# 1/z of a head pair by DMA broadcast in place of six transposes, and GpSimd made to wait for VectorE

## The chip, the cores and the metric

The kernel runs on one NeuronCore of a Trainium2 chip. The metric is the device time of one execution in microseconds (us), lower is better. A change of less than about 0.2% (1.3 us here) can hardly be told from none.

## The reference

Inputs are q, k and v of shape (2, 8, 768, 64), a random projection of 6 columns, and the weights of two feed-forward blocks of 512 channels. Attention is masked by hash buckets: a query sees only the keys whose projected sign bits equal its own. Each row is divided by its sum z.

```python
scores = np.where(mask, scale * q @ k.T, -1e9)
attn = np.exp(scores - scores.max(-1))
attn = attn / (attn.sum(-1) + 1e-9)
x = heads_side_by_side(attn @ v)             # (2, 768, 512)
h = relu(x @ w_in); u, v = halves(h)         # gated block
y = (u * (w_spatial @ layernorm(v) + b)) @ w_out
out = y + relu(layernorm(y) * g @ w1) @ w2
```

## The kernel before

The program has three parts. Part 0 is attention, with the projections of the first batch's gated block mixed in towards its end; parts 1 and 2 are the rest of the gated block and the second block. Attention works on 96 tiles of 128 queries, `order` in the code: 2 batches of 8 heads of 6 tiles. For a tile, TensorE makes the scores (`sc`), VectorE takes the masked minimum into `x` (signs are turned, so it is a row maximum), ScalarE takes the exponential in place and adds up the row sums into `z_sum`, TensorE transposes `x` in six blocks (`pt`), ScalarE and VectorE copy these to `e`, and after a head's sixth tile 24 matmuls (`po`) make the head's output, which two copies put into `xT`. `xT` holds channels on the partitions (two heads of 64 make one slice of 128) and queries on the columns. It is not yet divided by z.

The division is done for a pair of heads by two functions that `attn_step` calls. `summed` (line 895), one tile behind the pair's last `po`, takes 1/(z + 1e-9) into `zr`, where queries are on the partitions. `normalized` (line 902), three tiles behind, turns it: GpSimd spreads `zr` over 64 columns for each head (`zw`), TensorE transposes three blocks of 128x128 into `pz`, and VectorE multiplies `xT` by `pz`; that for both halves of the 768 queries, so six transposes for a pair and 48 for the eight pairs. Who reads `xT` is `x_split` (line 1038), which makes the operand `act_x` of the gated block's projections `pv`.

No instruction is issued in the order in which these functions call it. Each call is recorded as a job of the class `Plan`; `Plan.run` (line 298) plays the jobs against modelled costs, picks for each engine which job comes next, and `Plan.issue` (line 477) issues all jobs in the planned order of their start; each engine then runs its own in that order. So every edit deals the whole order anew, that of parts 1 and 2 too. Every job is issued by one line, 499, so the profile's rows are told apart by tile names. In the plan a VectorE job marked `shared` (its operands are all in SBUF) and a GpSimd job do not overlap; nothing makes the chip keep to that, since GpSimd runs ahead if its own inputs are there.

Loads of queries and keys (`qs`, `ks`), of `vv` and all reloads are issued by SyncE's queue (SP), in order; the raw weights and stores of weight pieces by ScalarE's queue. TensorE's outputs in attention go to `ps_s` (2 buffers of scores) and `ps_b` (4 banks, for `pt`, `po`, `pm` and `pz`).

Of the kernel before, what the change touches and what calls it, by code (L numbers as in the profile page):

```python
# [9 lines left out]
F32 = mybir.dt.float32  # L10
# [4 lines left out]
ALU = mybir.AluOpType  # L15
# [3 lines left out]
P = 128  # L19
# [124 lines left out]
class Job:  # L144
    def __init__(self, at, engine, part):
        self.at, self.engine, self.part = at, engine, part
        self.calls, self.after, self.busy, self.lag, self.bytes = [], set(), 0.0, 0.0, 0
        self.start = self.end = None
        self.shared = self.closed = False


# [18 lines left out]
class Plan:  # L170
# [4 lines left out]


    RUN = 6
    LOOK = 55
    EARLY = 20.0
    BULK = 14.0  # L180
# [117 lines left out]
    def run(self, late=None):  # L298
# [27 lines left out]
        def done(j):  # L326
            stack = [j]
            while stack:
                j = stack.pop()
                for h in heirs[j]:  # L330
                    if j.engine is None:
                        t = j.end
                    elif h.engine == j.engine and not j.bytes:
                        t = j.start + j.busy if h.engine in ("PE", "SP") else j.end + self.NEXT
                    else:
                        t = j.end + self.HOP.get(h.engine, 0.0)
                        if h.bytes and h.engine == "ACT":
                            t += self.SLACK
                    ready[h] = max(ready[h], t)
                    left[h] -= 1  # L340
                    if not left[h]:
                        if h.engine is None:
                            h.start = h.end = ready[h]
                            stack.append(h)
                        else:
                            known[h.engine].append(h)
# [5 lines left out]
        while todo:  # L352
            best = None
            for force, e in [(f, e) for f in (False, True) for e in engines]:
                if force and best:
                    break
                live = [p for p, n in parts[e].items() if n]
# [3 lines left out]
                c = [j for j in known[e] if j.part == part]  # L361
                if e != "PE" and not force:
                    c = [j for j in c if opened(j) is not None]
# [4 lines left out]
                t = max(free[e], min(ready[j] for j in c))  # L368
# [4 lines left out]
            t, e, c = best  # L373
# [103 lines left out]
    def issue(self):  # L477
        self.gates()
        self.settle()
        order = sorted((j for j in self.jobs if j.engine), key=lambda j: (j.part, j.start, j.at))  # L480
        engine = {"PE": "tensor", "ACT": "scalar", "DVE": "vector", "POOL": "gpsimd", "SP": "sync"}
        nc = self.tc.nc
        live = lambda x: x.real() if isinstance(x, View) else x
        opened = {}
        part = -1
        def opening(p):
            for pool in self.pools:
                if pool.part == p:
                    stack = opened.setdefault(pool.how.pop("till", None), ExitStack())
                    pool.real = stack.enter_context(self.tc.tile_pool(name=pool.name, bufs=pool.bufs, **pool.how))  # L490
        with self.tc.manual_schedule():
            for j in order:
                while part < j.part:
                    part += 1
                    if part in opened:
                        opened.pop(part).close()
                    opening(part)
                for op, args, kw in j.calls:
                    getattr(getattr(nc, engine[j.engine]), op)(*map(live, args), **{k: live(x) for k, x in kw.items()})  # L499
            for stack in reversed(list(opened.values())):  # L500
                stack.close()

# [2 lines left out]
def attn_moe_kernel(ctx: ExitStack, tc: tile.TileContext, qT, kT, v, proj, w_in, w_spT, b_sp, w_out, g_ln, w1, w2, out):  # L505
# [166 lines left out]
    xT = {}  # L672
# [221 lines left out]

    def summed(b, r):

        zr = ap.tile([P, NQT, 2], F32, tag="zr", name=f"zr_{b}_{r}")
        nc.vector.tensor_scalar(zr, z_sum[b][:, :, 2 * r : 2 * r + 2], 1e-9, None, op0=ALU.add)
        nc.vector.reciprocal(zr, zr)
        pairs[b, r]["zr"] = zr  # L900

    def normalized(b, r):

        zr = pairs[b, r]["zr"]
        for c in range(2):
            zw = ap.tile([P, 6, D], F32, tag="zw", name=f"zw_{b}_{r}_{c}", bufs=2)
            zc = zr[:, c * 3 : c * 3 + 3, :].rearrange("p a (h o) -> p (a h) o", o=1)
            nc.gpsimd.tensor_scalar(zw, zc.to_broadcast([P, 6, D]), 1.0, 0.0, op0=ALU.mult, op1=ALU.add)
            pz = ps_b.tile([P, 3, P], F32, tag="b", name=f"pz_{b}_{r}_{c}")
            for i in range(3):  # L910
                nc.tensor.transpose(pz[:, i, :], zw[:, 2 * i : 2 * i + 2].rearrange("p h d -> p (h d)"), ident)
            xs = xT[b][:, r, c * KC : (c + 1) * KC]
            nc.vector.tensor_tensor(xs, pz.rearrange("p a n -> p (a n)"), xs, op=ALU.mult)

    def attn_step(i):
# [11 lines left out]
            exps(*order[i + 1])  # L927
        if 0 <= i - PO < NT and order[i - PO][2:] == (NG - 1, GRP - 1):
            weighted(*order[i - PO][:2])
        for late, e in ((1, summed), (3, normalized)):  # L930
            n = i - PO - late
            if 0 <= n < NT and order[n][1] % 2 == 1 and order[n][2:] == (NG - 1, GRP - 1):
                e(order[n][0], order[n][1] // 2)
        n = i + 1 + QA
# [728 lines left out]
```

## Time and profile before

| | |
|---|---|
| time before, median of 3 runs | 649.05 us (648.55 to 649.79) |
| the profiled execution: its own time | 648.87 us |
| its span in the trace | 646.9 us |
| TensorE busy | 637.4 us (99%) |
| VectorE busy | 508.1 us (79%) |
| ScalarE busy | 326.4 us (50%) |
| GpSimd busy | 193.8 us (30%) |

The profiled execution's time is 1.97 us more than its span; that lies around the instructions. Matmuls are pipelined and their ends are modelled, so a busy TensorE may hold short pauses. PE is TensorE's matmul, PEld its weight load, DVE is VectorE, ACT ScalarE, POOL GpSimd, and SPq and ACTq are DMA issues on the queues of SyncE and ScalarE.

### The profile page before, as it was taken

The numbers are of one execution on the slowest core, as the hardware profiler recorded it, in microseconds if no ns is written. First come the engines' busy times: TensorE is split into PE (matmuls) and PEld (weight loads), VectorE is DVE, ScalarE is ACT, GpSimd is POOL, SyncE is SP. The second block draws the span as 40 slices with busy tenths as digits, with TensorE's granted clock in tenths as the row PEclk, the third lists the DMA queues.
The fourth block names the chain that finished last, engine by engine and source line by source line (L and its number), as shares of the span: only waits on it lengthen the run. The fifth ranks groups of instructions, "written<-read, shape, count | busy, mean of one in ns | idle before, by whom it ended". The sixth has DMA issues, their size and how long they took to land.

```text
span 646.9 us, 10064 instructions
## 1 busy us (share of the span) xinstructions
PE 637.4 (99%) x3506; PEld 521.4 (81%) x3506; DVE 508.1 (79%) x998; ACT 326.4 (50%) x650; POOL 193.8 (30%) x186
## 2 busy tenths in 40 slices
PE   8999999999999999989999999999999999999997
PEld 6776767777787777867888888899989999898896
DVE  5789888896888776856799544699998888999455
ACT  6887877785566554643465313464334233333110
POOL 3142433352556433122235100022223324232000
PEclk9999999999999999999999999999999999999999
DMA  6876676667755986764753222331354546461623
GB/s 154 206 192 154 179 177 175 163 144 236 230 158 152 302 231 195 221 253 148 271 206 105 73 67 98 130 96 53 113 182 144 193 150 223 138 226 56 230 88 147
DMA packets 62849, 107.67 MB, mean 166 GB/s; under 512 B 6912, under 2 KB 33232, under 8 KB 62288
## 3 DMA queue, kind: packets, MB, share of 16 engines
q1 hardware_dynamic: 43520, 71.78, 37.3%
q10 hardware_dynamic: 19280, 35.27, 16.7%
q8 instruction: 28, 0.46, 0.3%
q14 instruction: 21, 0.17, 0.1%
HBM read 63.31 MB, written 24.90 MB: 136 GB/s over the span
## 4 chain that ended last, share of the span: by engine, by line
PE 91%; DMA 3%; DVE 2%; ACT 1%; issue 1%; POOL 0%; SPq 0%; ACTq 0%; DVEq 0%; POOLq 0%
PE acc L499 20%; PE p L499 14%; PE pv L499 9%; PE sc L499 9%; PE po L499 9%; PE pt L499 8%; PE pg L499 7%; PE pc L499 5%; PE py L499 5%; DMA kept<-f64c_w 1%; DVE x L499 1%; DMA wst_sp<-in_w_spT 1%; PE pm L499 1%; PE warm L499 1%; PE px_c L499 1%
## 5 line engine op out<-in xcount | busy, mean ns | idle before, releaser
L499 PE MATMUL acc<-w,ch 128*128 128x512 f32 x576 | 143.0, 392 | 0.0
L499 PEld LDWEIGHTS acc<-w,ch 128*128 128x128 f32 x576 | 107.2, 188 | 18.9
L499 ACT ACTIVATE x<-x,nb 128x768 f32<-128x768 f32 x96 | 89.7, 935 | 23.6 <-DVE x L499 22.0
L499 PE MATMUL sc<-ks,qs 128*128 128x512 f32 (+3 forms) x384 | 93.9, 363 | 2.2 <-DVE x L499 2.2
L499 DVE TENSOR_SCALAR_CACHE_REDUCE x<-sc 128x768 f32<-128x768 f32 x96 | 90.7, 950 | 5.9 <-PE sc L499 2.7
L499 POOL TENSOR_TENSOR f64c_w<-f_w,f64c_w 128x512 f32<-128x512 f32 x32 | 45.1, 1408 | 153.0 <-issue 81.1
L499 PE MATMUL pt<-ident,x 128*128 128x128 f32 x576 | 80.8, 274 | 2.2 <-ACT y L499 1.9
L499 PEld LDWEIGHTS pt<-ident,x 128*128 128x128 f32 x576 | 66.5, 141 | 15.6 <-issue 4.2
L499 PEld LDWEIGHTS sc<-ks,qs 128*128 128x128 f32 (+1 forms) x384 | 63.4, 190 | 16.2 <-issue 4.8
L499 ACT ACTIVATE ch<-u 128x384 fp32r<-128x384 f32 x48 | 25.2, 526 | 80.8 <-DVE u L499 79.2
L499 PE MATMUL po<-e,vv 128*64 128x384 f32 x384 | 65.5, 490 | 0.0
L499 ACT ACTIVATE e<-pt 128x384 f32<-128x384 f32 x120 | 55.1, 485 | 18.4 <-PE pt L499 17.8
L499 DVE TENSOR_TENSOR u<-p,u 128x384 f32<-128x384 f32 x84 | 45.1, 549 | 16.8 <-PE p L499 16.5
L499 DVE COPY e<-pt 128x384 f32<-128x384 f32 x72 | 39.5, 552 | 15.6 <-PE pt L499 15.3
L499 PEld LDWEIGHTS po<-e,vv 128*64 128x64 f32 x384 | 26.2, 137 | 31.6 <-issue 29.6
L499 PE MATMUL p<-t,w 128*128 128x384 f32 x252 | 50.0, 337 | 0.0
L499 PE MATMUL p<-xh,w 128*128 128x384 f32 x252 | 48.8, 337 | 0.0
L499 DVE TENSOR_SCALAR f64c_w<-f64c_w 128x512 f32<-128x512 f32 x64 | 36.4, 569 | 13.4 <-ACT f64c_w L499 10.9
L499 PEld LDWEIGHTS p<-t,w 128*128 128x128 f32 x252 | 44.9, 188 | 2.3
L499 PEld LDWEIGHTS p<-xh,w 128*128 128x128 f32 x252 | 44.8, 188 | 1.9
L499 POOL TENSOR_TENSOR w<-f64c_w,w 128x512 fp32r<-128x512 f32 (+1 forms) x28 | 34.8, 1245 | 32.2 <-ACT w L499 25.7
L499 PE MATMUL pg<-vn,w_sp 128*128 128x512 f32 x180 | 43.9, 396 | 0.0
(155 smaller groups left out, 1029.0 us busy)
## 6 DMA issues: line engine op xcount, KB each, us to landing
f_w<-in_w ACTq DMA_DIRECT2D x32, 512.0 KB
ots<-y_dram SPq DMA_DIRECT2D x12, 768.0 KB
ks<-k SPq DMA_DIRECT2D x45, 192.0 KB
y_dram<-ots SPq DMA_DIRECT2D x30, 256.0 KB
qs<-q SPq DMA_DIRECT2D x30, 192.0 KB
wst_sp<-in_w_spT SPq DMA_DIRECT2D x12, 384.0 KB
w_out<-ws_out SPq DMA_DIRECT2D x2, 2048.0 KB
vv<-in_v SPq DMA_DIRECT2D x16, 192.0 KB
```

Of the source, the lines that this page charges most:

```text
L499: getattr(getattr(nc, engine[j.engine]), op)(*map(live, args), **{k: live(x) for k, x in kw.items()})
```

## The change

For seven of the eight pairs 1/z goes another way. `summed` writes `zr` with the head ahead of the tile number, by two small operations in place of one; one transpose turns all 12 columns at once into 12 rows of 128 (`pz`), VectorE copies them to `zt`, a DMA stores `zt` in DRAM (`zd`), and two DMAs load it back into `zb`, each with one head's 768 values broadcast to 64 partitions. `normalized` is then a single multiply of 768 columns, `xT` by `zb`, both in SBUF, and is called eight tiles behind in place of three. The last pair keeps the transposes; GpSimd's spreading takes four operations of half the size there, into one buffer that shares its place with `zb`. The planner adds 2 us to the end of a `zb` load when it plans its reader (`distant`).

Apart from that, `Plan.issue` gives a GpSimd instruction a wait for the last `shared` VectorE instruction issued ahead of it, if the plan lets it start less than 1.5 us after that one's end (or before it) and it does not wait for it already.

```diff
+    NEAR = 1.5
...
                         t = j.end + self.HOP.get(h.engine, 0.0)
+                        if j.distant:
+                            t += self.SLACK
...
                 for op, args, kw in j.calls:
-                    getattr(getattr(nc, engine[j.engine]), op)(...)
+                    res = getattr(getattr(nc, engine[j.engine]), op)(...)
+                    if j.shared:
+                        last = (j, res.ins)
+                    elif j.engine == "POOL" and op != "memset" and last and j.start - last[0].end < self.NEAR and last[0] not in j.after:
+                        self.tc.add_manual_dep(res.ins, last[1].name, sync, reason="apart")
...
     def summed(b, r):
-        zr = ap.tile([P, NQT, 2], F32, tag="zr", name=f"zr_{b}_{r}")
-        nc.vector.tensor_scalar(zr, z_sum[b][:, :, 2 * r : 2 * r + 2], 1e-9, None, op0=ALU.add)
+        zr = ap.tile([P, 2, NQT], F32, tag="zr", name=f"zr_{b}_{r}")
+        for h in range(2):
+            nc.vector.tensor_scalar(zr[:, h], z_sum[b][:, :, 2 * r + h], 1e-9, None, op0=ALU.add)
         nc.vector.reciprocal(zr, zr)
         pairs[b, r]["zr"] = zr
+        if (b, r) == (B - 1, H // 2 - 1):
+            return
+        rows = 2 * NQT
+        pz = ps_b.tile([P, GW], F32, tag="b", name=f"pz_{b}_{r}")
+        nc.tensor.transpose(pz[:rows, :P], zr.rearrange("p h a -> p (h a)"), ident)
+        zt = ap.tile([rows, P], F32, tag="zt", name=f"zt_{b}_{r}", bufs=1)
+        nc.vector.tensor_copy(zt, pz[:rows, :P])
+        zd = dram.tile([2, 1, S], F32, tag=f"zd_{b}_{r}", name=f"zd_{b}_{r}")
+        nc.sync.dma_start(out=zd.rearrange("h o (a q) -> (h o a) q", a=NQT), in_=zt)
+        zb = ap.tile([P, S], F32, tag="zw", name=f"zb_{b}_{r}", bufs=1)
+        for h in range(2):
+            nc.sync.dma_start(out=zb[h * D : (h + 1) * D], in_=zd[h].to_broadcast([D, S]))
+            plan.jobs[-1].distant = True
+        pairs[b, r]["zb"] = zb

     def normalized(b, r):
+        if "zb" in pairs[b, r]:
+            nc.vector.tensor_tensor(xT[b][:, r], pairs[b, r]["zb"], xT[b][:, r], op=ALU.mult)
+            return
...
-        for late, e in ((1, summed), (3, normalized)):
+        for late, e in ((1, summed), (3, normalized), (8, normalized)):
             n = i - PO - late
+            if late > 1 and (late == 8) == (n == NT - 1):
+                continue
```

## Rows read from the trace of the kernel before

**Rows 1.** The page, busy time of each engine, share of the span and instructions.

```profile
PE 637.4 (99%) x3506; PEld 521.4 (81%) x3506; DVE 508.1 (79%) x998; ACT 326.4 (50%) x650; POOL 193.8 (30%) x186
```

**Rows 2.** Busy time by stretch; last the granted clock, DMA share and GB/s.

```profile
17.40:145.40 128.00, 126.86 (x865) 92.18 (x864) 111.86 (x232) 104.06 (x228) 48.10 (x47) 1.00 0.69 174
145.40:306.60 161.20, 158.53 (x900) 120.45 (x899) 116.75 (x241) 86.49 (x172) 62.28 (x53) 1.00 0.69 212
306.60:646.90 340.30, 336.64 (x1668) 297.90 (x1667) 268.87 (x504) 123.83 (x233) 78.04 (x60) 1.00 0.41 143
```

**Rows 3.** Waits of TensorE's matmuls, whole span: us in total, times, longest.

```profile
PE sc L499 <- DVE x L499: 2.2, 6, 0.5
PE pt L499 <- ACT y L499: 1.9, 1, 1.9
```

**Rows 4.** Busy time by stretch of 20 us, where TensorE pauses; columns as above.

```profile
40.00:60.00 20.00, 19.53 (x133) 13.26 (x130) 16.69 (x33) 15.28 (x34) 8.85 (x9) 1.00 0.61 175
...
100.00:120.00 20.00, 19.45 (x136) 14.78 (x135) 17.88 (x38) 16.51 (x37) 5.50 (x6) 1.00 0.72 173
...
280.00:300.00 20.00, 18.14 (x102) 14.18 (x99) 13.27 (x28) 8.41 (x19) 2.73 (x3) 1.00 0.55 202
```

**Rows 5.** The chain that ended last, in order: start, us, what.

```profile
26.09 4.02 PE po L499 x24
...
72.58 0.66 PE pz L499 x6
73.24 1.19 PE sc L499 x6
...
80.46 4.02 PE po L499 x24
...
269.96 0.11 PE pt L499
```

**Rows 6.** Tile pz: ns min/median/max, first and last start, forms.

```profile
L499 PEld LDWEIGHTS pz<-ident,zw x48: 137/140/144, 46.4 to 306.2; 128*128 128x128 f32 x48
L499 PE MATMUL pz<-ident,zw x48: 270/272/330, 46.5 to 306.3; 128*128 128x128 f32 x48
L499 DVE TENSOR_TENSOR xT<-pz,xT x16: 547/552/558, 47.8 to 307.4; 128x384 f32<-128x384 f32 x16
```

**Rows 7.** Groups by form: busy us, mean ns, idle before them and releaser.

```profile
L499 DVE TENSOR_SCALAR zr<-z_sum 128x12 f32<-128x12 f32 x8 | 1.3, 162 | 0.0
...
L499 POOL TENSOR_SCALAR zw<-zr 128x384 f32<-128x384 f32 x16 | 9.6, 617 | 23.8 <-DVE zr L499 23.8
```

**Rows 8.** Tiles t, rx and f64c_w, VectorE: ns min/median/max.

```profile
L499 DVE TENSOR_TENSOR t<-rx,t x7: 944/946/949, 434.0 to 458.7; 128x768 fp32r<-128x768 f32 x7
L499 DVE TENSOR_TENSOR rx<-rx,rx x6: 944/948/2044, 429.5 to 452.8; 128x768 f32<-128x768 f32 x6
...
L499 DVE TENSOR_SCALAR f64c_w<-f64c_w x64: 393/421/1586, 189.4 to 590.8; 128x512 f32<-128x512 f32 x32, 128x512 uint32<-128x512 uint32 x32
```

**Rows 9.** Timeline at 49 us: start, us, engine, what, idle before it.

```profile
49.58 1.73 DVE L499 TENSOR_SCALAR f64c_v<-f64c_v 128x512 f32<-128x512 f32 x2
...
50.02 2.15 POOL L499 TENSOR_TENSOR k<-k 128x384 fp32r<-128x384 f32 x2 [2.15 <-PE pm L499]
```

**Rows 10.** The chain that ended last: its transfers.

```profile
100.75 4.79 DMA qs<-m
...
279.21 8.11 DMA kept<-f64c_w
```

**Rows 11.** Tile qs, SyncE's queue: ns of an issue, min/median/max.

```profile
L499 SPq DMA_DIRECT2D qs<-q x60: 473/628/1632, 13.4 to 260.8; - x60
L499 SPq DMA_DIRECT2D qs<-m x30: 784/792/2192, 15.5 to 261.5; - x30
```

**Rows 12.** Waits, SyncE's queue and then all engines: us, times, longest.

```profile
SPq L499 <- DMA y_dram<-ots: 12.8, 9, 4.7
...
ACT w L499 <- POOL f64c_w L499: 23.7, 16, 3.7
```

More of the change, by code (lines that the diff above doesn't have):

```diff
@@ L148, in __init__ @@
         self.start = self.end = None
+        self.distant = False
         self.shared = self.closed = False
@@ L484, in issue @@
         opened = {}
+        sync = mybir.DependencyInfo(mybir.DependencyClass.Sync, mybir.DependencyReason.DATA)
+        last = None
         part = -1
@@ L498, in issue @@
                 for op, args, kw in j.calls:
-                    getattr(getattr(nc, engine[j.engine]), op)(*map(live, args), **{k: live(x) for k, x in kw.items()})
+                    res = getattr(getattr(nc, engine[j.engine]), op)(*map(live, args), **{k: live(x) for k, x in kw.items()})
+                    if j.shared:
+                        last = (j, res.ins)
+                    elif j.engine == "POOL" and op != "memset" and last and j.start - last[0].end < self.NEAR and last[0] not in j.after:
+                        self.tc.add_manual_dep(res.ins, last[1].name, sync, reason="apart")
             for stack in reversed(list(opened.values())):
@@ L902, in normalized @@
+        for h in range(2):
+            nc.sync.dma_start(out=zb[h * D : (h + 1) * D], in_=zd[h].to_broadcast([D, S]))
+            plan.jobs[-1].distant = True
+        pairs[b, r]["zb"] = zb
     def normalized(b, r):
+        if "zb" in pairs[b, r]:
+            nc.vector.tensor_tensor(xT[b][:, r], pairs[b, r]["zb"], xT[b][:, r], op=ALU.mult)
+            return
         zr = pairs[b, r]["zr"]
+        both = ap.tile([P, S], F32, tag="zw", name=f"zw_{b}_{r}", bufs=1)
         for c in range(2):
-            zw = ap.tile([P, 6, D], F32, tag="zw", name=f"zw_{b}_{r}_{c}", bufs=2)
@@ L907, in normalized @@
-            zc = zr[:, c * 3 : c * 3 + 3, :].rearrange("p a (h o) -> p (a h) o", o=1)
-            nc.gpsimd.tensor_scalar(zw, zc.to_broadcast([P, 6, D]), 1.0, 0.0, op0=ALU.mult, op1=ALU.add)
+            zw = both[:, c * KC : (c + 1) * KC].rearrange("p (a h d) -> p a h d", a=3, h=2)
+            for h in range(2):
+                zc = zr[:, h, c * 3 : c * 3 + 3].rearrange("p (a o) -> p a o", o=1)
+                nc.gpsimd.tensor_scalar(zw[:, :, h], zc.to_broadcast([P, 3, D]), 1.0, 0.0, op0=ALU.mult, op1=ALU.add)
@@ L909, in normalized @@
             pz = ps_b.tile([P, 3, P], F32, tag="b", name=f"pz_{b}_{r}_{c}")
             for i in range(3):
-                nc.tensor.transpose(pz[:, i, :], zw[:, 2 * i : 2 * i + 2].rearrange("p h d -> p (h d)"), ident)
+                nc.tensor.transpose(pz[:, i, :], zw[:, i].rearrange("p h d -> p (h d)"), ident)
             xs = xT[b][:, r, c * KC : (c + 1) * KC]
```

## The prediction

> **What bounds the kernel now.** I read the busy times first: TensorE is busy 637.4 of 646.9 us [rows 1]. A busy TensorE need not be a full one, so I went on to the stretches. In the pure attention stretch (17 to 145 us) it pauses 1.14 of 128 us, in the mixed one (145 to 307 us) 2.67 of 161, after that only in the last 4 us; the granted clock is 1.00 throughout [rows 2]. The waits of its matmuls name 2.2 us for VectorE's masked scores and one wait of 1.9 us for ScalarE [rows 3], and stretches of 20 us place them: 0.47 us at 40 to 60, 0.55 at 100 to 120, 1.86 at 280 to 300 [rows 4]. Last, the chain that ended last runs through the transposes of the old division themselves: 72.58 + 0.66 = 73.24, where the scores begin with no gap [rows 5]. So in attention six `pz` transposes cost the end 0.66 us, 0.11 each, though one matmul's own duration is 0.27 [rows 6]: neighbours overlap, and the chain is the right price. In parts 1 and 2 TensorE waits for nothing, so whatever the new order does to VectorE or GpSimd there is worth nothing, unless it makes a wait that is not there now.
>
> **The change, part by part.** *Transposes removed.* Seven pairs lose six each: 7 x 0.66 = 4.62 us off the path [rows 5].
>
> *Transposes added.* One a pair, 12 columns of weights and 128 moving. No row shows such a shape. Above, it costs what a single full one costs on the chain, 0.11 us [rows 5]; below, nothing, if it falls into a pause. Weight loads of 128 columns take 140 ns [rows 6] and the moving side is as long as before, so I take the upper end: 7 x 0.11 = 0.77 us. It stands on TensorE until VectorE has made `zr`, with scores and `pt` behind it; the plan puts it where `zr` should be there, and a VectorE that runs late by half a microsecond would cost that much each time. I keep that for the range. Net: 4.62 - 0.77 = 3.85 us.
>
> The Trainium skill (TensorE: Matmul & The Clock Gate, Back-to-back issue gap) gives about 81 ns for a 128-column matmul in a stream of weight loads and matmuls. By that the 35 fewer would be worth 35 x 0.081 = 2.8 us; the trace has 110 ns for these 4-byte transposes, and the sum goes by the trace.
>
> *VectorE.* Out of each of seven pairs go two multiplies from PSUM, 2 x 0.552 = 1.10 us [rows 6]. In come: a second small addition, 0.16 [rows 7]; the copy of 12 rows of 128 from PSUM, between 0.16 (12 columns [rows 7]) and 0.55 (384 columns from PSUM [rows 6]), and I take 0.25, since 128 columns stand nearer the small end; one multiply of 768 columns with both operands in SBUF, 0.95 as the subtractions of the same shape [rows 8]. That is 1.36 - 1.10 = +0.26 us a pair, 1.8 in all; with the high copy +0.56. A pair takes (80.46 - 26.09) / 2 = 27.2 us [rows 5], and VectorE idles 16.1 of 128 us there [rows 2], so 3.4 us a pair: that is the cover, and I cost the 0.26 at nothing. If the cover were gone it is 1.8 us.
>
> *GpSimd.* 14 of 16 spreading operations of 0.62 us go [rows 7], 8.6 us; the last pair has four smaller ones, which wait only for `zr`. GpSimd idles 80 of those 128 us [rows 2] and TensorE does not wait for it, so this saves nothing by itself.
>
> *SyncE and the DMAs.* Three more issues a pair: 0.63 to 0.79 us each [rows 11], about 2 us. By the code the queue now issues 26 a pair (12 a head for `ks`, `qs`, `vv`, 2 raw loads), some 17 us of 27.2. The load of `zb` must stand at the head of SyncE's queue until the store of `zd` has landed, and behind it stand the next `qs` and `ks`, for which TensorE's scores wait. That stall is nothing if the plan is right about the landing; the nearest row, loads that wait for the kernel's own stores later on, has 12.8 us in 9 waits, 1.42 a wait and 4.7 at most [rows 12]. `qs` is asked for three tiles (3 x 2.27 = 6.8 us) ahead, so I take nothing on the path.
>
> *Eight tiles behind.* From `summed` to the multiply there are now 7 x 2.27 = 15.9 us. The way is 0.11 + 0.25, three issues (2 us) and two landings in series. With the longest landings on the chain, 4.79 and 8.11 [rows 10], it is 15.3; with 4.79 twice, 11.9. Both fit, the first barely. Who waits for `xT` is `x_split`; the first batch's starts at tile 60, and its last pair is now multiplied at step 57 where it was at 52, so that is still ahead. Nothing.
>
> *GpSimd waits for VectorE.* At 49.58 us two operations that take 0.42 each [rows 8] took 1.73, while a GpSimd subtraction started at 50.02 [rows 9]; the longest of that kind is 1586 ns against a median of 421 [rows 8]. The wait makes GpSimd the one that stands. What is queued behind it is the rest of its own queue, and ScalarE waits for GpSimd's weight sums, 23.7 us in 16 waits [rows 12]; TensorE does not. Where GpSimd held VectorE just ahead of a TensorE pause, the pause was 0.47 us at 40 to 60 [rows 4]. So the gain lies between 0 and some 0.5; and against it stands the tighter VectorE stage, whose pauses of 2.2 us [rows 3] grow if TensorE runs 2% faster. I let these cancel.
>
> Sum: 648.87 (the profiled execution, span 646.9 and 1.97 around it) - 3.85 = 645.0. The median of the runs is 0.18 above the profiled one, so 645.2.
>
> **The rivals.** *The saving turns into waits (no change).* VectorE is busy 111.9 of 128 us and hands each tile's scores on; if it sets the pace behind TensorE, 0.55 us a pair comes back as waits on `x` and the time stays 649.0. For it: nearly all short pauses are on `x` already. Against: it idles 3.4 us a pair. Chance 0.12.
>
> *The multiply is held by GpSimd (slower).* The old multiply read PSUM and never took over 558 ns in 16 [rows 6]; an operation with both operands in SBUF took 2044 in place of 948 once [rows 8]. Were each of seven held by 1.10 us on the path, 645.2 + 7.7 = 652.9; it undoes the gain from 3.85 / 7 = 0.55 us a pair on. Against: GpSimd is busy 38% of that stretch [rows 2], so a chance hit costs 0.38 x 0.55 = 0.2 us a pair, and the new waits keep it behind. Chance 0.07.
>
> The Trainium skill (SBUF — State Buffer, Who interferes with whom) says just this: a VectorE instruction with two SBUF inputs contends with a GpSimd instruction that reads SBUF, whoever starts first keeps the port pair for the whole instruction, and issue order decides who blocks. The stretched rows agree with it; that it speaks against moving the multiplier from PSUM to SBUF is why this rival has a chance of its own.
>
> *SyncE's queue stands (slower).* At 1.42 us a pair on the path, 645.2 + 9.9 = 655.1; at half of it 650.2; the deciding point is again 0.55 us a pair. For it: at 100 us TensorE paused 0.55 us after a `qs` transfer that took 4.79 us to land [rows 4, 10], so the lead of three tiles is not always enough. Against: that happened once in 15 heads. Chance 0.11.
>
> **How the numbers follow.** The forecast, 645.2, has 0.70. Its own range: down by the 1.9 us pause of rows 3, which the new order may drop, and the 0.5 us of the new waits, to 642.8; up by the VectorE cover, 1.8, to 647.0, or by a new pause like that of 1.9. The whole range takes in the no-change case and the milder ends of the slow ones: 642.5 to 649.8. Less than about 0.2% (1.3 us) cannot be told from no change. Faster: 0.70 and a bit of the mild ends, 0.72. Same: 0.12. Slower: 0.16.
>
> **What would show it.** Right: 13 `pz` transposes; the three issues a pair on SyncE; the single multiply at about 0.95 us; attention over about 3.9 us earlier with TensorE's pauses as short as before; parts 1 and 2 as long as before (340 us). Wrong: rows in which `sc` waits for `x` over 6 us in total; a VectorE wait for the `zb` transfer; SyncE waits on `zd` followed by scores that wait for `qs`; or TensorE pauses after 307 us behind a GpSimd weight piece, where there are none now.

## The result and the profile after

The changed kernel took 656.35 us in the median of four runs (654.71 to 660.97), the kernel before 648.8 on the same chip: a ratio of 1.011, 95% interval 1.0082 to 1.0138. It is slower by 7 us where 3.85 us of gain were forecast, and the time lies above the range. The profiled execution took 655.42 us with a span of 653.6. Ratios leave out an execution that took over 1.5% longer than the fastest of its kernel; only e18 below has such, two of twelve.

The page of the changed kernel, busy time of each engine, answers to [rows 1]:

```profile
PE 637.2 (97%) x3471; PEld 518.4 (79%) x3471; DVE 508.5 (78%) x1006; ACT 326.9 (50%) x650; POOL 182.8 (28%) x174
```

The instructions are those the change promised: TensorE has 35 fewer, VectorE's sum is the same within 0.4 us, GpSimd has 11.0 us less. TensorE's busy time fell by 0.2 us and not by 35 x 0.11 = 3.85, but this says little of the transposes: the mean granted clock of this execution was 0.995, for 1.000 before, and at that clock about 3.3 us (653.6 x 0.005, an estimate) are added to work that TensorE does without a pause. Busy time by stretch, with the columns of [rows 2]:

```profile
17.40:145.40 128.00, 124.06 (x830) 88.19 (x828) 109.72 (x227) 100.71 (x221) 42.90 (x38) 1.00 0.72 185
145.40:306.60 161.20, 157.14 (x873) 120.19 (x873) 121.20 (x251) 89.59 (x175) 60.30 (x50) 0.98 0.72 212
306.60:653.60 347.00, 341.95 (x1694) 299.50 (x1690) 266.55 (x504) 123.95 (x234) 75.07 (x60) 1.00 0.42 144
```

TensorE now pauses 3.94 us in the first stretch (1.14 before) and 4.06 in the second (2.67), and in the second the granted clock is no longer whole. TensorE's waits over the whole span answer to [rows 3]:

```profile
PE sc L505 <- DMA qs<-q: 2.4, 2, 1.5
PE sc L505 <- DVE x L505: 1.9, 3, 1.0
PE pv L505 <- DVE e L505: 1.8, 1, 1.8
...
PE pt L505 <- ACT x L505: 1.2, 3, 0.6
PE pz L505 <- DVE xT L505: 1.1, 1, 1.1
```

VectorE's masked scores `x`, on which the first rival staked, cost no more than before (1.9 for 2.2 us). New are waits for `qs` transfers, and a place where VectorE is late.

**The place near 208 us.** The timeline of the changed kernel, first TensorE's rows, then ScalarE's with its queue, then VectorE's (start, duration, what, idle before it; L505 is the line that issues every instruction of this kernel):

```profile
206.37 0.95 PE L505 MATMUL sc<-ks,qs 128*128 128x512 f32 x4
208.43 0.28 PE L505 MATMUL pz<-ident,zr 128*12 128x128 f32 x1 [1.10 <-DVE xT L505]
...
211.92 5.49 PE L505 MATMUL pv<-w_u,act_x 128*128 128x512 f32 x12 [1.84 <-DVE e L505]
...
218.78 2.94 PE L505 MATMUL pv<-w_u,act_x 128*128 128x512 f32 x12
...
196.74 0.40 ACTq L505 DMA_DIRECT2D f_w<-in_w  x1
...
206.12 0.66 ACT L505 ACTIVATE f64c_w<-f_w 128x512 f32<-128x512 f32 x1 [5.09 <-DMA f_w<-in_w]
206.81 0.48 ACT L505 ACTIVATE xT<-po 64x384 f32<-64x384 f32 x1
207.32 0.60 ACT L505 ACTIVATE xT<-pv 128x512 f32<-128x512 f32 x1
207.81 0.48 ACT L505 ACTIVATE e<-pt 128x384 f32<-128x384 f32 x1
...
200.58 0.19 DVE L505 RECIPROCAL zr<-zr 128x12 f32<-128x12 f32 x1
...
206.89 0.43 DVE L505 TENSOR_SCALAR f64c_w<-f64c_w 128x512 f32<-128x512 f32 x1 [5.88 <-ACT f64c_w L505]
...
207.81 0.56 DVE L505 COPY xT<-po 64x384 f32<-64x384 f32 x1
...
211.30 0.56 DVE L505 COPY e<-pt 128x384 f32<-128x384 f32 x1
```

ScalarE stood (waited with nothing to do) 5.09 us for a weight piece (`f_w`, raw; `f64c_w` is ScalarE's copy of it) that was asked for at 196.74 and taken up at 206.12. Behind it in ScalarE's order stood copies that attention needs. VectorE, whose order had steps on the same piece next, stood 5.88 us for ScalarE's copy, and its own copies for attention came after those steps. The new transpose `pz` did not wait for `zr`, which was ready at 200.77: the trace names VectorE's copy of `po` into `xT`, and `pz` and `po` share the banks of `ps_b`. The `pv` matmuls waited for VectorE's copy `e`. So TensorE paused 2.94 us in two parts. Then twelve matmuls, which take 2.94 us at 218.78, took 5.49. The stretches of 2 us show why (columns as in [rows 2]):

```profile
208.00:210.00 2.00, 1.57 (x11) 1.32 (x11) 1.97 (x7) 0.29 (x1) 0.00 (x0) 1.00 0.90 270
210.00:212.00 2.00, 0.16 (x2) 0.09 (x1) 1.97 (x5) 1.15 (x2) 0.00 (x0) 0.70 1.01 397
212.00:214.00 2.00, 2.00 (x5) 1.61 (x6) 2.00 (x5) 1.41 (x2) 1.59 (x2) 0.50 0.97 336
214.00:216.00 2.00, 2.00 (x6) 1.52 (x6) 0.72 (x3) 1.54 (x5) 2.00 (x3) 0.50 0.98 213
216.00:218.00 2.00, 2.00 (x11) 1.60 (x9) 0.00 (x0) 0.56 (x2) 2.00 (x3) 0.59 1.16 246
218.00:220.00 2.00, 2.00 (x13) 1.70 (x11) 1.52 (x3) 0.43 (x2) 1.05 (x1) 1.00 1.11 269
```

From about 211 to 217 us the granted clock was at half, the lower of its two levels, which is all that this execution's clock was short of (the 3.3 us above): the pause of 2.9 us was paid about twice.

**The places where `qs` is late.** SyncE's queue and TensorE at 81 to 91 us of the changed kernel:

```profile
81.35 1.16 SPq L505 DMA_DIRECT2D zb<-zd  x2
...
84.36 1.32 SPq L505 DMA_DIRECT2D qs<-q  x2
...
90.50 0.73 PE L505 MATMUL sc<-ks,qs 128*128 128x512 f32 x2 [1.48 <-DMA qs<-q]
```

The two `zb` loads, which fill 128 rows of 768 four-byte columns (393 KB), go out 3 us ahead of a `qs` move that the scores need at 89. There was no such pause there before. At 105 us the pause is 0.91, for `qs`; before it was 0.55 [rows 4], and there the trace names VectorE's `x`, which ended at 105.61, 0.07 us after the `qs` move of [rows 10]. That the `zb` loads make `qs` late is not shown at this place, only likely: in the eight traces below and here with whole `zb` loads TensorE waits 0.6 to 4.0 us for `qs`, in the other twelve 0 to 1.8.

**Where the time is lost.** Starts of TensorE's first `po` of a head, or of its first or last matmul of a kind, taken from the two traces (us; heads are counted from 0):

```
                          before    after
po of head 0               26.02    25.02
po of head 8              134.75   134.54
po of head 13             250.29   256.05
last pv                   346.89   351.27
last pv to last acc       295.97   297.66
```

At head 8 the changed kernel is ahead by 0.2 us, where four pairs should have given 2.2. It was ahead by 1.0 us at the first `po`, before any division, so it lost 0.8 on the way. From head 8 to 13 it loses 6.0, then it wins back 1.4, and the stages after attention are 1.7 us longer.

### The profile page after: what moved, and what is told of

It is laid out like the page before. It is cut to its first block, busy times and chain, and to the rows that moved or that the text cites. A ratio compares the mean times of both kernels' runs of the same rounds, so it can differ in the third digit from the quotient of the medians.

```text
span 653.6 us, 10037 instructions
## 1 busy us (share of the span) xinstructions
PE 637.2 (97%) x3471; PEld 518.4 (79%) x3471; DVE 508.5 (78%) x1006; ACT 326.9 (50%) x650; POOL 182.8 (28%) x174
## 5 line engine op out<-in xcount | busy, mean ns | idle before, releaser
L505 PE MATMUL acc<-w,ch 128*128 128x512 f32 x576 | 143.8, 393 | 0.0
L505 PEld LDWEIGHTS acc<-w,ch 128*128 128x128 f32 x576 | 107.1, 188 | 18.9 <-DVE ch L505 0.3
L505 ACT ACTIVATE x<-x,nb 128x768 f32<-128x768 f32 x96 | 89.7, 936 | 28.0 <-DVE x L505 24.4
L505 PE MATMUL sc<-ks,qs 128*128 128x512 f32 (+3 forms) x384 | 93.8, 363 | 4.4 <-DMA qs<-q 2.4
L505 DVE TENSOR_SCALAR_CACHE_REDUCE x<-sc 128x768 f32<-128x768 f32 x96 | 90.3, 949 | 4.5 <-PE sc L505 3.1
L505 PE MATMUL pt<-ident,x 128*128 128x128 f32 x576 | 81.0, 275 | 1.2 <-ACT x L505 1.2
L505 POOL TENSOR_TENSOR f64c_w<-f_w,f64c_w 128x512 f32<-128x512 f32 x32 | 43.3, 1352 | 137.2 <-issue 67.7
L505 PEld LDWEIGHTS sc<-ks,qs 128*128 128x128 f32 (+1 forms) x384 | 63.4, 190 | 18.7 <-DVE x L505 3.6
L505 PEld LDWEIGHTS pt<-ident,x 128*128 128x128 f32 x576 | 66.9, 141 | 14.0 <-issue 3.2
L505 ACT ACTIVATE ch<-u 128x384 fp32r<-128x384 f32 x48 | 25.2, 525 | 88.0 <-DVE u L505 83.5
L505 ACT ACTIVATE e<-pt 128x384 f32<-128x384 f32 x120 | 55.7, 486 | 21.4 <-PE pt L505 21.2
L505 PE MATMUL po<-e,vv 128*64 128x384 f32 x384 | 65.5, 491 | 0.0
L505 DVE TENSOR_TENSOR u<-p,u 128x384 f32<-128x384 f32 x84 | 45.0, 548 | 12.7 <-PE p L505 12.3
L505 DVE TENSOR_SCALAR f64c_w<-f64c_w 128x512 f32<-128x512 f32 x64 | 33.9, 530 | 22.6 <-ACT f64c_w L505 20.6
L505 PEld LDWEIGHTS po<-e,vv 128*64 128x64 f32 x384 | 26.2, 137 | 31.4 <-issue 29.6
L505 DVE COPY e<-pt 128x384 f32<-128x384 f32 x72 | 39.4, 550 | 14.4 <-PE pt L505 14.0
L505 PE MATMUL p<-t,w 128*128 128x384 f32 x252 | 50.4, 338 | 0.1
L505 PE MATMUL p<-xh,w 128*128 128x384 f32 x252 | 49.0, 338 | 0.2 <-DVE u L505 0.2
L505 PEld LDWEIGHTS p<-t,w 128*128 128x128 f32 x252 | 44.8, 188 | 3.1 <-DVE u L505 0.7
L505 PEld LDWEIGHTS p<-xh,w 128*128 128x128 f32 x252 | 44.7, 188 | 2.4 <-DVE u L505 0.6
L505 POOL TENSOR_TENSOR w<-f64c_w,w 128x512 fp32r<-128x512 f32 (+1 forms) x28 | 35.8, 1280 | 33.0 <-ACT w L505 16.9
L505 PE MATMUL pg<-vn,w_sp 128*128 128x512 f32 x180 | 44.0, 397 | 0.0
```

Of the source, the lines that this page charges most:

```text
L505: res = getattr(getattr(nc, engine[j.engine]), op)(*map(live, args), **{k: live(x) for k, x in kw.items()})
```

## The experiments

Each run is compared with runs of the kernel before on the same chip. As a ratio moves by 0.001, the time moves by 0.65 us. Part of the spread is the clock, whose mean is on record for every execution: of the 127 of the kernel before with these runs, the 90 at 0.999 or 1.000 took 649.1 us in the median and the 37 at 0.994 to 0.997 took 651.3. A trace shows one execution.

```
run                                      median  before  ratio  95% interval
changed kernel                           656.35  648.80  1.0110 1.0082-1.0138
e1  change, no GpSimd waits              657.06  649.26  1.0103 1.0052-1.0155
e2  before, GpSimd waits only            651.87  649.26  1.0027 1.0005-1.0049
e3  old order, spread and waits          661.70  649.26  1.0183 1.0144-1.0222
e4  old order, spread                    657.94  649.26  1.0142 1.0093-1.0191
e5  change, no zd/zb transfers           653.84  649.73  1.0069 1.0030-1.0108
e6  old order, no zd/zb transfers        651.27  649.73  1.0009 0.9988-1.0031
e7  old order, zb of 8 columns           654.61  649.73  1.0068 1.0047-1.0089
e8  before, dealt anew                   648.60  649.73  0.9981 0.9966-0.9996
e9  before, 16 of 48 transposes          648.85  649.60  0.9978 0.9958-0.9997
e10 before, 96 transposes                651.19  649.60  1.0014 0.9995-1.0033
e11 change, one copy moved               656.51  649.60  1.0081 1.0053-1.0110
e12 change, dealt anew                   654.16  649.60  1.0057 1.0033-1.0082
e13 e11 and one load moved               653.05  649.34  1.0045 1.0026-1.0064
e14 e5 and that load moved               651.49  649.34  1.0027 1.0011-1.0043
e15 before, that load moved forward      649.48  649.34  1.0001 0.9984-1.0018
e16 e9 without the multiplies            649.19  649.34  0.9992 0.9978-1.0006
e17 e13, no GpSimd waits                 650.69  649.19  1.0024 1.0004-1.0045
e18 e14, no GpSimd waits                 650.56  649.19  1.0017 0.9993-1.0041
```

**The waits of GpSimd, alone and left out (e1, e2).** e1 leaves the added dependence out of the changed kernel, e2 puts it into the kernel before; the order of the engines stays in both.

```diff
-elif j.engine == "POOL" and op != "memset" and last and j.start - last[0].end < self.NEAR and ...:
-    self.tc.add_manual_dep(res.ins, last[1].name, sync, reason="apart")
```

> The changed kernel in its own order, without GpSimd's added waits. Three theories for the 7.5 us lost. Order: the planner dealt a new order that runs into late transfers around 90, 105 and 200 us; then this stays at 654 to 658. Transfers: the broadcast loads crowd the DMA engines; 654 to 658 too. Waits: GpSimd, made to wait, hands its results on late; then this comes back to 649 or below.

> The kernel before in its own order, with GpSimd's added waits alone (40 more of its instructions wait for VectorE). Order and transfers: 648 to 650, since neither is touched. Waits: 651 or more.

The waits cost the kernel before 1.8 us by the ratio (0.3 to 3.2), and leaving them out of the changed one gives back nothing that its runs can tell (1.0103 beside 1.011). They are not the bulk of the loss, and no gain shows either. In e1 the pauses stand elsewhere: 1.62 us at 209 us and 2.98 at 222.

**The division spread by DMA in the old order (e3, e4).** All work that both kernels share is issued in the order of the kernel before; only the steps of the division are exchanged, the transpose in its old place, the store planned 1.8 us, the load 5.5 us and the multiply 12 us later. e3 has GpSimd's waits, e4 not.

```diff
+first = record(Plan(tc), True, *args)     # the old functions
+first.gates(); first.settle()
+second = record(Plan(tc), False, *args)   # the changed ones
+second.gates(); second.place(first)       # shared work where the first plan has it
+second.issue()
```

> Everything common to both kernels keeps the order of the kernel before; only the steps of the division are exchanged in place, GpSimd's waits are added. Order: the saving of TensorE shows, 645 to 646. Transfers: 651 or more. Waits: 651 or more.

> As the held order with the exchanged division, but without GpSimd's waits. Order: 645 to 646. Transfers: 651 or more. Waits: 645 to 646, which together with a slow run with the waits would put it on them.

So it is not the planner's new order alone: with the old one, and the transfers put in by hand, the change is worse (the intervals of e3 and e4 overlap, so the waits can't be told there). A wait of SyncE's queue in e4 (total, times, longest), and then its timeline:

```profile
SPq L544 <- DMA zd<-zt: 8.5, 4, 3.4
...
101.44 0.46 SPq L544 DMA_DIRECT2D zd<-zt  x1
...
103.57 0.62 SPq L544 DMA_DIRECT2D qs<-q  x1
105.93 1.12 SPq L544 DMA_DIRECT2D zb<-zd  x2
107.15 0.80 SPq L544 DMA_DIRECT2D qs<-m  x1
```

Here `zb` stands at the head of the queue until the store `zd` has landed, 4.5 us after its issue, and the mask rows of `qs` behind it are late: this is the third rival, but in an order that the changed kernel's planner avoids: there the loads go out 1.7 to 81 us behind their stores (26 for the first, 54.96 and 81.35), and the trace shows no wait of SyncE for `zd`.

**The transfers left out or made small (e5, e6, e7).** e5 is the changed kernel and e6 is e4 with the stores `zd` and the loads `zb` not issued; the multiply takes `xT` by itself. e7 is e4 with loads of 8 columns, the multiply taking one of them.

```diff
+if j.bytes and named(j.calls[0][2].get("out"), "zd_", "zb_"):
+    continue
...
-nc.sync.dma_start(out=zb[h * D : (h + 1) * D], in_=zd[h].to_broadcast([D, S]))
+nc.sync.dma_start(out=zb[h * D : (h + 1) * D, 0:8], in_=zd[h, :, 0:8].to_broadcast([D, 8]))
```

> The changed kernel in its own order with GpSimd's waits, but the 7 stores of zd and 14 loads of zb are left out and the multiply takes xT by itself, so the division is not done. Transfers (they crowd the queue and the DMA engines): 645 to 647, with the pauses at 90, 105 and 200 us gone. Order: 652 to 656, since the pause at 200 us stands behind a weight piece, not behind zb. A result between would split the loss.

> The held order without GpSimd's waits and without the zd and zb transfers, the multiply again xT by itself. Both theories give 645 to 646, the saving of TensorE that was forecast. If it stays at 650 or more, the saving does not exist even with the order of before, and something else than the transfers takes it.

> The held order without GpSimd's waits, with all 21 transfers and their waits, but each zb load brings 8 columns in place of 768 (2 KB in place of 196 KB; the multiply takes one column broadcast, so the division is wrong). If the bytes in the DMA engines do the harm: 645 to 647. If SyncE's queue, standing until zd has landed, does it: 652 to 658 as with full loads.

TensorE's waits in e5:

```profile
PE pt L512 <- ACT xT L512: 2.8, 1, 2.8
PE pt L512 <- ACT y L512: 1.8, 1, 1.8
...
PE sc L512 <- DVE x L512: 1.3, 3, 0.7
```

The waits for `qs` are down to 0.3 us, and head 8 starts at 132.34, 2.4 us ahead of the kernel before, of which 0.65 was there at the first `po`. (e14 below is the same kernel up to 200 us; in its trace one `qs` wait is 1.76 us and head 8 starts at 133.68, so one trace does not settle this.) A pause of 2.8 us near 219 us stays, and the time is still 1.0069. In the old order all the loss goes with the transfers (1.0142 to 1.0009), half of it with their bytes (e7), though SyncE's queue waits as long for `zd` in e7 as in e4 (8.0 and 8.5 us); TensorE's waits for `qs` are 2.1 us in e4's trace, 0.9 in e7's, none in e6's. Yet e6 shows no saving either, which no theory so far explained: with 35 transposes fewer and no transfers it should have come to about 646.

**Another order of the same work (e8, e12).** One constant of the planner, for the kernel before and for the changed one:

```diff
-    NEXT = 0.03
+    NEXT = 0.035
```

> The kernel before with one modelled cost changed by 5 ns (NEXT 0.035 for 0.03): the same instructions, another order. If a newly dealt order alone can cost what was lost, this lands 2 us or more from 649; if the order hardly matters, within 1 us.

> The changed kernel dealt anew by one constant of the planner (0.035 for 0.03 us between two dependent instructions of an engine), which leaves all the work as it is; the same step moved the kernel before by -1.1 us only. If the loss is the change's own (transfers that crowd the loads, waits of GpSimd), this order is as slow: 653 to 659 us. Rival: the loss is one unlucky order with its stand of ScalarE at 200 us, and another order comes to 647 to 651 us.

By the ratio the kernel before moved by -1.2 us and the changed one by -3.4, and it stays slower. It has the pause again, 2.98 us at 222 us, and one of 2.70 for `qs` at 120.

**What a transpose is worth (e9, e10, e16).** The kernel before in its own order, with the three transposes of a `pz` tile issued once (e9, the first block taken three times), or twice each (e10); e16 is e9 without the multiplies.

```diff
+if calls[0][0] == "transpose" and pz(calls[0][1][0]):
+    calls = calls[:1]          # e10: calls + calls
+if op == "tensor_tensor" and pz(args[1]):
+    args = (xs, args[1].base[:, 0:1].to_broadcast([P, 3, P]), xs)   # e16: continue
```

> The kernel before in its own order on every engine, with one of the three 128-column transposes of each pz tile left in place and the other two left out (32 of 48 are gone, nothing is added; the multiply takes the first block of 128 columns three times, so the output isn't the reference's). It prices the step of the prediction that called TensorE's instructions the chain that sets the time. If they are, 32 x 0.11 = 3.5 us go: about 645.3 us beside 648.8. Rival: in attention TensorE only fills the time that ScalarE and VectorE set, and what it is spared it waits; then the time stays within 0.8 us of the kernel before. The held order without transfers, which came to 651.3 us instead of about 646, speaks for the rival; 644.5 to 646.5 would leave the loss in that kernel to its VectorE steps or its SyncE steps.

> The kernel before in its own order, with each of the 48 transposes of pz issued twice (the output is the reference's). It prices the same step by adding. TensorE's chain sets the time: 48 x 0.11 = 5.3 us more, about 654. Rival (TensorE has room in attention): less than 2 us more, about 649 to 651. If the run with a third of them gains little and this one costs the full 5.3 us, then the kernel stands where TensorE and the two other engines are level: adding costs, taking away gives nothing back.

> The kernel before in its own order with a third of the pz transposes, as in the run that left out two of three, and without the 16 multiplies of VectorE that take them up (16 x 0.55 = 8.8 us of VectorE; the output isn't divided by z). If VectorE sets the pace of attention, so that the 32 transposes left out gave back nothing, part of those 8.8 us comes back now: 641 to 646 us. Rival (the pace is a chain of dependent steps in turn through TensorE, VectorE and ScalarE, of which the division is no part): within 1 us of the run with the multiplies, 648 to 649.5.

This is the term of the sum that failed. 32 transposes fewer gave 1.4 us by the ratio (0.7 by the medians) where 3.5 were due, 48 more cost 0.9 (1.6), where 5.3 were due: 0.02 to 0.04 us each. The intervals, 0.2 to 2.7 us less and 0.3 less to 2.1 more, hold neither 3.5 nor 5.3. Among executions at a granted clock of 0.999 or 1.000 alone, e9 is 1.0 us below the kernel before and e10 2.0 above: 0.03 and 0.04 each. How it goes away is seen when the same matmul is looked up in two traces. The table gives, for the first tile of each pair, the start of the matmul just before it and just after it, less the start of the same matmul in the kernel before:

```
pair's pz at   e9 before it, after it   e10 before it, after it
 46.5            0.01   -0.43             0.13    0.79
 72.4           -0.15   -0.33             0.02    0.68
 99.2           -0.10   -0.23             0.72    1.06
127.3            0.11   -0.11             0.84    1.17
163.2            0.11   -0.33             1.12    1.77
211.8           -0.32   -0.72             1.81    2.47
265.8            0.06   -0.38             1.12    1.77
305.7            1.59    1.15             1.39    2.04
```

On the spot the chain's price is right: two tiles with two transposes less each are 0.44 us, and 0.66 for six more. But by the next pair TensorE has mostly lost again what it gained, and caught up in part with what it was charged. It does so in its waits: from 20 to 307 us they are 3.8 us before, 5.0 in e9 and 2.4 in e10, where the four on VectorE's `x` (1.6 us before) are gone. The last one stands at 288.6 us. The timeline of the kernel before, that of e9, and a stretch of 20 us of e9 (the same in [rows 4] has the clock at 1.00):

```profile
288.60 0.55 PE L499 MATMUL pt<-ident,x 128*128 128x128 f32 x3 [1.86 <-ACT y L499]
...
288.56 0.55 PE L508 MATMUL pt<-ident,x 128*128 128x128 f32 x3 [2.17 <-ACT y L508]
...
280.00:300.00 20.00, 17.83 (x91) 13.77 (x88) 11.59 (x23) 6.87 (x15) 2.62 (x2) 0.91 0.46 166
```

With 28 transposes less TensorE goes on at the same time. It waits for ScalarE's `y`, and the chain that ended last leads from there to the transfer `kept`, 8.11 us before [rows 10] and 8.41 in e9. Behind that wait the clock fell in e9's traced execution, to 0.50 from 290 to 292 us; the last row of the table shows this and not the transposes. Leaving out VectorE's 8.8 us as well gives nothing more that the runs can tell (e16), so the division's VectorE steps don't set that pace.

**The stand of ScalarE at 200 to 222 us (e11, e13, e14, e15).** e11 is the changed kernel with the copy of the second kept weight piece behind the three instructions it held up, and VectorE's steps on that piece as much later. e13 is e11 with one more instruction moved, SyncE's load of `w_out` from `ws_out` (2,048 KB), back behind the two `ks` moves; e14 moves it in e5, e15 moves it forward by four places in the kernel before.

```diff
 self.gates()
 self.settle()
+self.put_off("f64c_w1_", 1, 4.5)   # e11, e13: the second copy, and what it hands on
+self.shift("ws_out", 14.0)         # e13, e14; e15: -6.0
```

> The changed kernel with one instruction moved: ScalarE's copy of the second kept weight piece, for which ScalarE stood 5.09 us at 201 to 206 us of the changed kernel's trace, comes after the three instructions that stood behind it (two copies to xT and an exponential), and VectorE's six steps on that piece come after the work that stood behind them; every other instruction keeps its place. If that stand and the fall of the granted clock behind it are the order's part of the loss, 3 us of pause and up to 3 us of clock come back: 650.5 to 653.5 us beside 656.4, and the granted clock is 0.9 or more in 200 to 220 us. Rival: something else is as late there (the softmax of that head, VectorE), the pause only moves and the time stays within 1 us of 656.4.

> The kernel of the run before with the moved weight piece (itself the changed kernel with one copy of ScalarE moved), with one more instruction moved: SyncE's load of w_out from ws_out (2,048 KB), which every traced order of the change issues at 202 to 207 us ahead of the qs and ks moves and of the third kept piece (the kernel before: at 210 us, behind them), goes five places back, behind the two ks moves. If that load is what keeps the third piece 11 us on its way and ScalarE standing 4.6 us at 217 us, the 3.0 us pause of TensorE at 222 us and the fall of the clock to 0.91 behind it go: 651 to 653 us beside 656.5. Rival: the piece is late for another reason (the transfers of the division, or ScalarE's own queue), the pause stays and so does the time, within 1 us.

> The changed kernel's order without the stores zd and the loads zb (the multiply takes xT by itself, so the division isn't the reference's), with the same single load put five places back on SyncE. If transfers and that load are together the loss, the 2.76 us pause at 219 us and the clock behind it go: 649 to 650.5 us beside the 653.8 of the kernel without transfers, which is the kernel before, with no gain left from the transposes. Rival of more hope: the transposes' saving shows as well, 646 to 648 us. Rival: no change, 653 to 654.5.

> The kernel before with this one instruction moved: SyncE's load of w_out (2,048 KB) goes four places forward, ahead of the three qs moves and of wst_sp, as in the changed kernel; all else stands as before. If its place is the cause of the stand at 220 us, the kernel before now shows it too: a pause of TensorE of 2 to 3 us near 220 us behind ScalarE, a granted clock under 0.95 behind it and 3 to 5 us more, 652 to 654 us. Rival: the load is harmless here and the time stays within 1 us of 649.3.

In e11 the stand only moved to the third piece. The timeline of e11, rows of SyncE's queue, of ScalarE with its queue, and of TensorE:

```profile
207.63 0.34 SPq L534 DMA_DIRECT2D w_out<-ws_out  x1
...
209.81 0.41 ACTq L534 DMA_DIRECT2D f_w<-in_w  x1
...
221.19 0.66 ACT L534 ACTIVATE f64c_w<-f_w 128x512 f32<-128x512 f32 x1 [4.55 <-DMA f_w<-in_w]
...
222.39 0.93 PE L534 MATMUL pt<-ident,x 128*128 128x128 f32 x6 [3.00 <-ACT xT L534]
```

The piece asked for behind the load of 2 MB took 11.4 us to be taken up. With that load behind `qs` and `ks`, the timeline of e13, ScalarE with its queue and then SyncE's queue:

```profile
211.47 0.41 ACTq L553 DMA_DIRECT2D f_w<-in_w  x1
218.20 0.67 ACT L553 ACTIVATE f64c_w<-f_w 128x512 f32<-128x512 f32 x1
...
215.30 0.55 SPq L553 DMA_DIRECT2D w_out<-ws_out  x1
```

Busy time by stretch of 20 us in e13, columns as in [rows 2]:

```profile
200.00:220.00 20.00, 20.00 (x114) 15.05 (x112) 13.73 (x34) 11.63 (x24) 9.80 (x9) 1.00 0.82 231
220.00:240.00 20.00, 19.54 (x116) 14.12 (x115) 17.62 (x32) 11.73 (x23) 8.47 (x7) 1.00 0.87 275
```

The third piece is taken up 6.7 us after it was asked for, TensorE's pause is gone and the clock whole there: 3.5 us in the medians, 2.3 by the ratio. (Elsewhere in this trace the clock did fall, at 122 to 126 us, behind a wait of 1.63 us for `qs`.) e14 gained 2.4 us by the medians over e5, less than was expected; there ScalarE still stands 4.36 us for the second piece and TensorE pauses 1.84, besides the 1.76 for `qs` at 118 us. But e15 fell: in the kernel before the same load may go out at 203 us, ahead of the third piece, which then takes 8.5 us and pauses TensorE 0.8 us, and the time does not change. So the load is a cause in the company that the new order gives it (the `qs` and `ks` moves and the piece all within 5 us behind it), not by its place alone.

**The mended order without GpSimd's waits (e17, e18).** The edit of e1, made to e13 and e14.

> The kernel of e13 (the changed kernel with one weight piece's copy and the w_out load moved) without the added waits of GpSimd on VectorE; the order of every engine is that of e13. The weight stages after attention were 1.2 us longer in e13 than in the kernel before (from the last pv to the last acc 297.21 for 295.96 us) and as long as before in e1, which has no waits. If the waits cost there, 1 to 1.5 us go: 651.5 to 652.1 us, and 296.0 us from the last pv to the last acc. Rival (the order of those stages costs it, not the waits): 653 us and 297 us.

> The kernel of e14 (the changed kernel's order without the division's transfers, with the w_out load moved; not the reference's division) without the added waits of GpSimd. With the transfers, the load's place and the waits gone, what is left of the change is the transposes' saving and VectorE's 0.26 us a pair more. If the account is whole, it stands where the kernel before stands, less the 0.5 to 1 us that the transposes are worth: 648.3 to 650 us. Rival: the order itself holds a further cost that has no name yet, 650.5 to 651.5 us.

In e17 the last `pv` to the last `acc` takes 296.04 us, for 297.21 in e13, 295.97 before and 295.97 in e1. In all traces of the changed order it is 296.57 to 297.66 with the waits (six) and 295.97 to 296.78 without (three), so the waits probably lengthen these stages by about 1 us there; the time fell by 1.4 us (1.0045 to 1.0024, with intervals that overlap). e18 can't be told from the kernel before, nor from e17. Its median is 650.56 over all twelve executions, and 649.80 over the ten that its ratio takes, which is inside what a whole account was to give. What is left of e17's loss is mostly clock: its four executions at 0.999 or 1.000 took 649.3 us in the median, level with the 18 of the kernel before there (649.2), but eight of its twelve were below that and took 653.0, where five of 23 of the kernel before were. One cause of a pause in its trace is the added transpose's bank: `pt` waited 1.79 us at 217 us for the copy `zt` of `pz`.

## Why the prediction was wrong

Two steps failed, and the time is about 11 us from the forecast. One is a term of the sum, the transposes removed, which accounts for 2.3 to 3.2 us of that. The other is what the sum put at nothing: the order, the transfers and the waits, the order being the largest by far (below).

*The transposes removed* is the term that failed, with 3.85 us net as its sum. The price of 0.11 us on the chain [rows 5] was right on the spot and wrong as a price of the end; e9 and e10 measured 0.02 to 0.04 us a transpose, so the 35 fewer were worth 0.7 to 1.6 us. The prediction took the chain for TensorE's because it runs through the transposes without a gap. But the same chain passes through transfers [rows 10], and ahead of 288.6 us TensorE waited longer in e9 for what the longest of them held up. The first rival had this in it, "the saving turns into waits", but gave it to VectorE and expected it in long waits on `x`. VectorE's steps of the division were tested (e16) and are not it; its other work was not, and which chain sets attention's pace is not settled. The traces of the changed order without the transfers show a saving at head 8 (0.7 to 1.8 us from the first `po` on in e5, e14 and e18), the old order (e6, e9) shows none there, so what it is worth may hang on the order too.

*The transposes added* took what was forecast on the spot: behind five of the seven the next matmul starts 0.11 us later, behind two 0.03, as behind the last of an old six (72.96 to 72.99). Their dependence on `zr`, kept "for the range", did not bite; what did, by 1.10 us at 208 us, was the bank that they need.

*VectorE* came out as worked out: 0.16 + 0.27 + 0.95 - 1.10, with 0.27 for the copy where 0.25 was taken. Tile `zb` on VectorE:

```profile
L505 DVE TENSOR_TENSOR xT<-zb,xT x7: 939/953/2062, 88.9 to 288.6; 128x768 f32<-128x768 f32 x7
```

*The multiply held by GpSimd* (second rival) happened in two of seven, 2.06 us at 138.47 and 1.75 at 280.45, in spite of the waits; GpSimd instructions had begun 0.3 and 0.4 us earlier and ended at 139.72 and 281.38. No pause of TensorE follows from it directly. The Trainium skill (SBUF — State Buffer, Who interferes with whom) says that the one that starts first keeps the port; these two rows agree.

*GpSimd* lost 11.0 us of work and nothing came of it, as said.

*SyncE and the DMAs* were costed at nothing on the path, the second error. The queue did not stand for `zd` in the changed kernel. That the bytes of `zb` cost time is shown in the old order (e4 to e7, with the same waits for `zd`: 4.8 us); that they do it by crowding the `qs` moves, a mechanism that the prediction didn't name, is likely and not shown. Leaving the transfers out is worth 2.7 us by the ratio in the changed order (e5, with intervals that overlap), 8.6 in the old one (e4 to e6), where the queue stands as well, and 0.5 to 1.2 once the order is mended (e13 to e14, e17 to e18).

*GpSimd's waits* were to cancel out; they cost 1.8 us alone (e2, 0.3 to 3.2).

*The order* was not costed at all, and is the largest part of the loss. The sum took the work out of a schedule as if the rest stood still, but the planner deals all engines anew: ScalarE's weight pieces came out where they are taken up before they can be there, in all five traces of the change ahead of the mending (5.09, 4.55, 4.96 and 4.35 us of one stand in the changed kernel, e11, e12 and e5; 7.5 us in two in e1). The kernel before has such a stand too, 4.78 us at 287 us, ahead of its pause of 1.86. Two instructions moved by hand (e11, e13) brought the ratio from 1.011 to 1.0045. With the waits out as well it is 1.0024, and without the transfers 1.0017.

So the 7 us are, in round numbers by these ratios, 4 for the order's stand with its fall of the clock, 1.5 for the waits, and the rest for transfers and whatever else the smaller saving doesn't cover. These shares depend on the order in which they are taken out, and the last two are each near what a run can tell. Seen another way, about half of the loss is clock: the four executions of the changed kernel had mean clocks of 0.991 to 0.995, which is 3.3 to 5.9 us of them (span x (1 - clock), an estimate), and none had its clock whole. No version with the spread division came out ahead of the kernel before; the fastest that divides by z was the kernel before dealt anew (e8, 0.9981).

## What to carry to other kernels

A gapless chain through an instruction does not price it for the end: take some of them out, or issue them twice, in a fixed order, and use that price. When a planner deals all engines anew, compare the new order's loads and the first instruction that waits for each of them before counting a local saving. A transfer that no engine waits for can still have a price (e4 to e7); leave it out, or make it small, to learn it. Compare the clocks of many executions, too: a change that adds short pauses may cost nothing in some and microseconds in others.

## What the runs showed of the hardware

A short pause can cost twice. In the changed kernel pauses of 1.10 and 1.84 us, 3.5 us apart, were followed by about 6 us at a granted clock of 0.50 to 0.70, and twelve `pv` matmuls took 5.49 us instead of 2.94. It does not follow each time: after one pause of 1.84 us ahead of the same matmuls they took 3.06 us in e14, at a granted clock of 1.00, and 4.62 in e18, at 0.50 from 210 to 212 us. In the twenty traces of this case 12 of 26 pauses of 1.5 us or more, the warm-up's left out, were followed by such a fall, the shortest of them 1.53 us (e17); others of up to 2.71 (e7) were not. What decides it is not shown.

A load of one piece of w1 (512 KB), there at most 6.7 us after it was asked for in e13, with `w_out`'s 2,048 KB asked for 3.8 us behind it (ScalarE was busy until it took the piece up), took 11.4 us in e11 with them 2.2 us ahead of it.
